# Seven products in place of eight in the first layer of five experts, with sums of w1 on GpSimd and running sums in PSUM

## The chip, the cores and the metric

The kernel runs on one core of a Trainium2 chip. The metric is the time of one execution in microseconds on the device, median of several runs; lower is better. Engines are called PE (TensorE, matmuls), ACT (ScalarE), DVE (VectorE), POOL (GpSimd) and SP (queue that issues most of the DMA).

## What is computed

An attention block with a decaying state (RWKV), whose result is regrouped into 3072 rows of 384, and then a mixture of eight experts in which every expert gets exactly 384 rows. Everything is float32.

```python
for t in range(S):                       # B=4, H=8, S=768, D=48
    cur = einsum('bhd,bhe->bhde', u * k[t], v[t])
    y[t] = einsum('bhd,bhde->bhe', r[t], state + cur)
    state = w * state + einsum('bhd,bhe->bhde', k[t], v[t])
x = y as (3072, 384)
logits = x @ w_gate                      # (3072, 8)
# all (row, expert) pairs from the largest logit down: the row goes to the expert
# if the row is free and the expert has fewer than 384 rows
for e in range(8):                       # w1 (8, 384, 1024), w2 (8, 1024, 384)
    h = maximum(x[mask_e] @ w1[e], 0)
    out[mask_e] = h @ w2[e]
```

## The kernel before

**Stages.** The first 125 us or so are attention (class `Mild`, an order written out by hand). The assignment of rows ("the walk", class `Assignment`) finds one expert's 384 rows after another: short steps on DVE with small matmuls on PE between them (tiles `counts`, `some_ps`, `list_ps`, `st_ps`; most of its DVE operations go through a helper at L930). The experts are computed in the order in which the walk finds them; n counts them in that order. Expert 0 is partly computed beside the end of attention (`early`), n = 1 to 7 by `Experts.run`, and at the end a piece of 128 rows that was put off (n = 8).

**One expert.** `fetch` gathers its 384 rows by three indirect DMAs of POOL (L1511) and loads w2 and w1 (1.5 MB each, L1504, in this order, on SP's queue). The buffers of weights and rows alternate between two pools, `turns[n % 2]`. `turn` transposes the rows to `xT`, three blocks of 128 inner indices by 384 rows (L1526), through PSUM and ACT (L1527). `hidden` computes the first layer transposed: for each of eight pieces of 128 hidden units three matmuls over the inner blocks (weights: a 128 x 128 block of w1; moving operand: 384 columns of xT) sum up in one bank of PSUM, and ACT takes the maximum with zero into `hid` (L1539, L1541).

**Second layer.** For n = 1 to 5, rows 0 to 255 go through `seven`: the product of a 2 x 2 division of the hidden rows and a 2 x 2 division of w2 by seven products of sums (Winograd's form of Strassen's method) in place of eight. The blocks are named h0 to h3 and w0 to w3; the sums are S1 to S4 (of hid) and T1 to T4 (of w2). Rows 256 to 383 go through `result` in the ordinary way. For n = 6 and 7 (`many`) all 384 rows go through `fifteen`: fifteen products in place of eighteen, with sums H and W. `sums_of` makes all these sums on DVE (L1591, 128 x 512, or 128 x 768 for T), `products` runs the matmuls into groups of one bank (`p_ps`, L1614), copies each group to `res` on ACT (L1618) and combines the products on DVE (L1623). Rows leave by indirect DMA of POOL (L1635).

**What sets the order.** Within the experts' part the Tile framework's planner puts every engine's instructions into a fixed order, by estimated readiness and with earlier code first; each engine then runs its own list in that order and waits by semaphores. `progress` says at which fraction of an expert's work (0 to 1 hidden layer, 1 to 2 second layer) a further step of the walk is put into the program (`due`); the list of steps is the generator `later`. The next expert's `fetch` is asked for at the head of the loop in `run`, its `turn` ahead of the last `result` (or, for `many`, when the list of `due` runs out).

**Banks of PSUM.** Three pools of two banks each: `ps_t` (transposes, `xT_ps`), `ps_h` (hidden layer, `h_ps`), `ps_o` (second layer, `p_ps` and `o_ps`, which share the tag `o_ps`).

## Time and profile before

| what | value |
|---|---|
| median of 3 runs | 398.21 us (397.88 to 398.33) |
| the profiled execution, its own time | 398.63 us |
| its span, first to last instruction | 396.9 us |
| granted clock of PE | 0.996 |
| PE busy | 381.1 us, 96% of the span |
| DVE, ACT, POOL busy | 267.4, 161.3, 137.9 us |
| first-layer passes of 384 columns (L1539) | 336, busy 114.9 us |
| second-layer passes of 192 columns (L1614) | 280 |
| second-layer passes of 128 columns (L1614) | 240 |

The page shows one execution. Busy times of different engines overlap; [...] the mean of one pass is longer than the distance from one pass to the next. A float32 matmul appears as two passes, each with its own load of weights (PEld).

### The profile page before, as it was taken

The page shows a single profiled execution, that of the slowest core. Times are in us where ns is not written, and L with a number is a line of the kernel's source. Part 1 is how long each engine was busy: PE and PEld are TensorE (multiplying, and loading weights), DVE is VectorE, ACT ScalarE, POOL GpSimd, SP SyncE. Part 2 cuts the span into 40 slices and gives each one's busy share as a digit, 9 for nine tenths or more (in the row PEclk, how much of TensorE's full clock was granted, in tenths as well). Part 3 has the DMA queues.
Part 4 walks back from the last instruction along what each step waited for, and adds up shares of the span by engine and source line. Part 5 has one row for each costly group of instructions (what it writes and reads, how often), then busy time and mean ns, then how long its engine had stood idle before and what let it go on. Part 6 is the DMA issues. An engine that isn't in the chain of part 4 may idle for free.

```text
span 396.9 us, 8692 instructions
## 1 busy us (share of the span) xinstructions
PE 381.1 (96%) x3243; PEld 289.4 (73%) x3243; DVE 267.4 (67%) x934; ACT 161.3 (41%) x429; POOL 137.9 (35%) x173
## 2 busy tenths in 40 slices
PE   7899999999999998999999999999999999999993
PEld 5678888888877764587578569558757857966981
DVE  6755777576885787967839819979578663952620
ACT  4997878888873311222222122221222222222220
POOL 7888877666732022031121120302303221040020
PEclk9999999999999999999999999999999999999998
DMA  9999999897692164641460650109209173370010
GB/s 121 158 184 205 197 201 171 151 177 153 125 327 81 42 247 169 215 164 40 152 246 12 220 208 2 60 0 334 84 21 359 57 281 120 99 300 2 2 61 26
DMA packets 95331, 57.29 MB, mean 144 GB/s; under 512 B 77232, under 2 KB 89520, under 8 KB 95280
## 3 DMA queue, kind: packets, MB, share of 16 engines
q1 hardware_dynamic: 91936, 47.21, 47.4%
q0 software_dynamic: 3104, 9.44, 6.7%
q8 instruction: 27, 0.44, 0.5%
q14 instruction: 24, 0.20, 0.2%
q10 hardware_dynamic: 240, 0.00, 0.0%
HBM read 47.20 MB, written 9.44 MB: 143 GB/s over the span
## 4 chain that ended last, share of the span: by engine, by line
PE 73%; DVE 10%; issue 4%; ACT 3%; POOL 3%; DMA 3%; SPq 1%; POOLq 0%; another core or an unknown queue 0%; DVEq 0%; ACTq 0%
PE h_ps L1539 26%; PE p_ps L1614 14%; PE o_ps L1641 7%; PE y_ps L542 6%; PE g_ps L504 4%; PE e_h_ps L1709 3%; PE kv_ps L521 2%; DMA krs<-in_k_dram 2%; PE kT_ps L458 2%; ACT AT L495 2%; PE x_ps L591 2%; PE lg_ps L571 2%; PE xT_ps L1526 2%; DVE W L1591 2%; PE rT_ps L458 1%
## 5 line engine op out<-in xcount | busy, mean ns | idle before, releaser
L1539 PE MATMUL h_ps<-xT,w 128*128 128x384 f32 (+1 forms) x384 | 120.8, 467 | 0.6 <-ACT e_o_sb L1721 0.6
L1539 PEld LDWEIGHTS h_ps<-xT,w 128*128 128x128 f32 x384 | 66.7, 190 | 39.1 <-issue 2.2
L1541 ACT ACTIVATE hid<-h_ps 128x384 f32<-128x384 f32 (+1 forms) x64 | 29.7, 464 | 91.3 <-PE h_ps L1539 79.9
L495 ACT ACTIVATE AT<-ident,dd 128x128 f32<-128x128 f32 x192 | 59.1, 391 | 2.0 <-DVE dd L448 1.8
L1511 POOL DMA_INDIRECT xg<-x_rows,tok x22 | 21.9, 997 | 88.0 <-issue 36.0
L1635 POOL DMA_INDIRECT out_dram<-o_all,to x16 | 17.6, 1103 | 99.2 <-DVE o_all L1623 66.8
L508 DVE COPY_PREDICATED AT<-mask,g_ps 128x512 f32<-128x512 uint8 x48 | 32.6, 732 | 12.1 <-PE g_ps L504 10.7
L1618 ACT COPY res<-p_ps 128x384 f32<-128x384 f32 (+2 forms) x28 | 13.2, 473 | 60.5 <-PE p_ps L1614 58.4
L1641 PE MATMUL o_ps<-w,hid 128*128 128x384 f32 x96 | 33.1, 488 | 0.0
L504 PE MATMUL g_ps<-rT,kT 48*128 48x128 f32 x384 | 27.9, 284 | 0.7 <-DVE AT L508 0.6
L436 POOL TENSOR_TENSOR kss<-krs,wk 128x384 f32<-128x384 f32 x24 | 24.3, 1017 | 8.0 <-DVE krs L340 5.5
L504 PEld LDWEIGHTS g_ps<-rT,kT 48*128 48x128 f32 x384 | 23.4, 187 | 4.0 <-PE unread_ps L418 0.5
L542 PE MATMUL y_ps<-AT,vts 128*64 128x128 f32 x384 | 25.7, 276 | 0.0
L443 POOL TENSOR_TENSOR rk<-rk,u_bc 128x384 f32<-128x384 f32 x24 | 24.2, 1007 | 1.9
L442 POOL TENSOR_TENSOR rk<-krs 128x384 f32<-128x384 f32 x24 | 24.6, 1024 | 0.2 <-DMA krs<-in_r_dram 0.2
L1641 PEld LDWEIGHTS o_ps<-w,hid 128*128 128x128 f32 x96 | 17.2, 190 | 9.5 <-issue 0.2
L542 PEld LDWEIGHTS y_ps<-AT,vts 128*64 128x64 f32 x384 | 20.6, 137 | 1.2 <-issue 0.7
L1614 PE MATMUL p_ps<-T,S 128*128 128x192 f32 x120 | 20.9, 328 | 0.0
L1591 DVE TENSOR_TENSOR H<-hid 128x512 f32<-128x512 f32 x12 | 7.9, 687 | 19.1 <-ACT hid L1541 19.1
L560 ACT COPY x<-y_ps 128x512 f32<-128x512 f32 x24 | 14.0, 585 | 14.6 <-PE y_ps L542 14.6
L1614 PEld LDWEIGHTS p_ps<-T,S 128*128 128x128 f32 x120 | 19.6, 190 | 0.1
L1614 PE MATMUL p_ps<-w,hid 128*128 128x192 f32 (+1 forms) x112 | 19.0, 316 | 0.0
(303 smaller groups left out, 684.9 us busy)
## 6 DMA issues: line engine op xcount, KB each, us to landing
w<-in_moe_w_dram SPq DMA_DIRECT2D x18, 1536.0 KB, 6.8
krs<-in_k_dram SPq DMA_DIRECT2D x24, 192.0 KB, 4.4
krs<-in_r_dram SPq DMA_DIRECT2D x24, 192.0 KB, 4.9
vts<-in_v_dram SPq DMA_DIRECT2D x24, 192.0 KB
x_rows<-xr SPq DMA_DIRECT2D x24, 192.0 KB, 3.0
xg<-x_rows,tok POOLq DMA_INDIRECT x22, 4.2
out_dram<-o_all,to POOLq DMA_INDIRECT x16, 2.7
out_dram<-o_sb,to POOLq DMA_INDIRECT x5
```

The costliest lines, as they stand in the source:

```text
L436: self.nc.gpsimd.tensor_mul(self.kss[:, n % self.NS].rearrange("p (g h) d -> p g h d", g=2)[:, :, :, 0:D], src, self.wk.rearrange("p (g h) ...
L442: nc.gpsimd.tensor_mul(rk, self.krs[:, n % self.NK, 1, 0:H, 0:D], self.krs[:, n % self.NK, 0, 0:H, 0:D])
L443: nc.gpsimd.tensor_mul(rk, rk, self.u_bc)
L495: nc.scalar.mul(AT[:, z, a, :], self.ident, dd[:, h:h + 1])
L504: nc.tensor.matmul(g_ps[:, z, a, :], kT[rows, a, :], rT[rows, a, :], start=True, stop=True)
L508: nc.vector.copy_predicated(out=AT[:, z], mask=self.mask.unsqueeze(1).to_broadcast([128, HP, T]), data=g_ps[:, z])
L542: nc.tensor.matmul(yv[q * PD:(q + 1) * PD, o // 2, o % 2, :], lhsT, rhs, start=(o // 2, q) not in seen, stop=stop, skip_group_check=True)
L1511: nc.gpsimd.indirect_dma_start(out=xg[:, c, :], out_offset=None, in_=x_dram[0:within, :], in_offset=bass.IndirectOffsetOnAxis(ap=tok[:, c: ...
L1539: nc.tensor.matmul(h_ps[:, 0:m], w1[:, f, ts(j, 128)], xT[:, f, 0:m], start=(f == 0), stop=(f == KD - 1))
L1541: nc.scalar.activation(hid[:, j, 0:m], h_ps[:, 0:m], AF.Relu)
L1614: nc.tensor.matmul(ps[:, q, :], left[a][:, j, :], right[b][:, j, :], start=(j == 0), stop=(j == KF // 2 - 1))
L1641: nc.tensor.matmul(o_ps, hid[:, j, ts(c, 128)], w2[:, j, :], start=(j == 0), stop=(j == KF - 1))
```

## The change

Five experts (`FIRST_BY_SEVEN`: n = 2, 3, 5, 6, 7) compute the first layer by `hidden_by_seven`. Inner blocks 0 and 1 of xT and of w1, halves of the rows (192 each, a0 to a3) and halves of the hidden units (512 each, b0 to b3) make a 2 x 2 by 2 x 2 product that is done by seven products; the third inner block (d0, d1 by c0, c1) is multiplied in the ordinary way, in the same accumulations. The hidden units are done in two passes p, each with half of them. One bank (A) takes P1, P6, P7 and P4 one after another as a running sum that is copied out by ACT between them; bank B takes P5 and P3, bank C takes P2. DVE adds what was kept to what stands in the bank for three of the four blocks.

The sums of w1 (T1 to T4, 128 x 512) are made on POOL during the second layer of the expert ahead, those of xT (S1 to S5, 128 x 192) on DVE after its `turn`.

The second layer's `seven` is rewritten with running sums in the same manner: P1, P6, P7 and P4 in one bank, P5 and P3 in another, P2 in a bank of `ps_t`; `turn` is now called ahead of P4. Four copies of ACT, one copy of the last block and three additions of DVE take the place of four copies and seven additions. T4 changes its sign.

For `fifteen` the products, the sums H and the combinations are the same in another order, and the two sums that were made after half of the hidden layer are made after all of it.

```diff
--- before.py
+++ after.py
...
+            self.first = pool("f_first", 1, **how)
...
+        def weight_sums(self, w1):
+            H = F // 2
+            at = {f"b{2 * k + f}": w1[:, k, ts(f, H)] for k in range(2) for f in range(2)}
+            at.update({f"c{f}": w1[:, 2, ts(f, H)] for f in range(2)})
+            for name, a, op, b in (("T1", "b1", SUB, "b0"), ("T2", "b3", SUB, "T1"), ("T3", "b3", SUB, "b1"),
+                                   ("T4", "b2", SUB, "T2")):
+                t = self.first.tile([128, H], F32, name=f"first_{name}")
+                nc.gpsimd.tensor_tensor(out=t, in0=at[a], in1=at[b], op=op)
+                at[name] = t
+            return at
+
+        def row_sums(self, xT):
+            H = CAP // 2
+            at = {f"a{2 * i + k}": xT[:, k, ts(i, H)] for i in range(2) for k in range(2)}
+            at.update({f"d{i}": xT[:, 2, ts(i, H)] for i in range(2)})
+            for name, a, op, b in (("S1", "a2", ADD, "a3"), ("S2", "S1", SUB, "a0"), ("S4", "a1", SUB, "S2"),
+                                   ("S5", "d0", SUB, "d1"), ("S3", "a0", SUB, "a2")):
+                t = self.first.tile([128, H], F32, name=f"first_{name}")
+                nc.vector.tensor_tensor(out=t, in0=at[a], in1=at[b], op=op)
+                at[name] = t
+            return at
+
+        FIRST = {"P1": (("a0", "b0"),), "P2": (("a1", "b2"), ("d0", "c0")), "P5": (("d1", "c1"), ("S1", "T1")),
+                 "P6": (("S2", "T2"),), "P7": (("S3", "T3"),), "P3": (("S5", "c1"), ("S4", "b3")),
+                 "P4": (("d1", "c0"), ("a3", "T4"))}
+        FIRST_ORDER = ("P1", 0), ("P2", 0), ("P5", 0), ("P6", 0), ("P1", 1), ("P7", 0), ("P3", 0), ("P4", 0), \
+            ("P5", 1), ("P6", 1), ("P2", 1), ("P7", 1), ("P3", 1), ("P4", 1)
+
+        def hidden_by_seven(self, x, w, progress):
+            hid = self.h.tile([128, KF, CAP], F32, name="hid")
+            Q, H = KF // 4, CAP // 2
+            banks, kept = {}, {}
+
+            def bank(p, which):
+                if (p, which) not in banks:
+                    pool, name, tag = {"A": (self.ps_h, "h_ps", None), "B": (self.ps_o, "hb_ps", "o_ps"),
+                                       "C": (self.ps_t, "hc_ps", "xT_ps")}[which]
+                    banks[p, which] = pool.tile([128, Q, H], F32, name=name, tag=tag or name), True
+                ps, fresh = banks[p, which]
+                banks[p, which] = ps, False
+                return ps, fresh
+
+            def keep(p, name, ps):
+                t = self.sums.tile([128, Q, H], F32, name=f"kept_{name}", tag=f"sum_False_{5 + 3 * p + len(kept) % 3}")
+                nc.scalar.copy(t, ps)
+                kept[name, p] = t
+
+            def block(p, i, f, src):
+                nc.scalar.activation(hid[:, ds(f * KF // 2 + p * Q, Q), ts(i, H)], src, AF.Relu)
+
+            def added(p, i, f, name, other):
+                t = kept[name, p]
+                nc.vector.tensor_tensor(out=t, in0=t, in1=other, op=ADD)
+                block(p, i, f, t)
+
+            for step, (name, p) in enumerate(self.FIRST_ORDER):
+                ps, fresh = bank(p, {"P2": "C", "P5": "B", "P3": "B"}.get(name, "A"))
+                pairs = self.FIRST[name]
+                for a, b in pairs:
+                    for q in range(Q):
+                        nc.tensor.matmul(ps[:, q, :], w[b][:, ts(p * Q + q, 128)], x[a], start=fresh,
+                                         stop=(a, b) == pairs[-1], skip_group_check=True)
+                        fresh = False
+                if name in ("P1", "P5", "P6"):
+                    keep(p, name, ps)
+                elif name == "P2":
+                    added(p, 0, 0, "P1", ps)
+                elif name == "P7":
+                    added(p, 1, 1, "P5", ps)
+                elif name == "P3":
+                    added(p, 0, 1, "P6", ps)
+                else:
+                    block(p, 1, 0, ps)
+                progress((step + 1) / len(self.FIRST_ORDER))
+            return hid
...
         SEVEN_EARLY = (("S3", "h0", SUB, "h2"),)
         SEVEN_LATE = (("S1", "h2", ADD, "h3"), ("S2", "S1", SUB, "h0"), ("S4", "h1", SUB, "S2"))
-        SEVEN = ((("p1", "h0", "w0"), ("p2", "h1", "w2")), (("p7", "S3", "T3"), ("p5", "S1", "T1")),
-                 (("p6", "S2", "T2"), ("p3", "S4", "w3")), (("p4", "h3", "T4"),))
-        SEVEN_OUT = ((("o0", "p1", ADD, "p2"),), (), (("u2", "p1", ADD, "p6"), ("u3", "u2", ADD, "p7"),
-                     ("u4", "u2", ADD, "p5"), ("o1", "u4", ADD, "p3"), ("o3", "u3", ADD, "p5")),
-                     (("o2", "u3", SUB, "p4"),))
-        EARLY_SUMS = (("H1", "h0", ADD, "h2"), ("H11", "h0", SUB, "h4"))
-        HID_SUMS = (("H8", "h1", ADD, "h3"), ("H7", "h1", SUB, "h0"), ("H9", "h1", SUB, "H11"),
-                    ("H3", "h5", SUB, "H9"), ("H0", "h1", ADD, "h2"), ("H6", "h3", ADD, "h5"),
+        SEVEN = (("P1", "h0", "w0"), ("P2", "h1", "w2"), ("P5", "S1", "T1"), ("P6", "S2", "T2"), ("P3", "S4", "w3"),
+                 ("P7", "S3", "T3"), ("P4", "h3", "T4"))
+        HID_SUMS = (("H7", "h1", SUB, "h0"), ("H8", "h1", ADD, "h3"), ("H6", "h3", ADD, "h5"), ("H1", "h0", ADD, "h2"),
+                    ("H11", "h0", SUB, "h4"), ("H9", "h1", SUB, "H11"), ("H3", "h5", SUB, "H9"), ("H0", "h1", ADD, "h2"),
                     ("H5", "H11", ADD, "H6"), ("H2", "h2", SUB, "H6"), ("H12", "H2", ADD, "h4"))
...
-        PRODUCTS = ((("p4", "h4", "w1"), ("p1", "H1", "w2"), ("p11", "H11", "W11"), ("p10", "h5", "w4")),
-                    (("p8", "H8", "w5"), ("p13", "h1", "W13"), ("p7", "H7", "W7"), ("p9", "H9", "W9")),
-                    (("p3", "H3", "w3"), ("p0", "H0", "W0"), ("p14", "h2", "W14"), ("p5", "H5", "W5")),
+        PRODUCTS = ((("p10", "h5", "w4"), ("p13", "h1", "W13"), ("p7", "H7", "W7"), ("p8", "H8", "w5")),
+                    (("p4", "h4", "w1"), ("p14", "h2", "W14"), ("p1", "H1", "w2"), ("p11", "H11", "W11")),
+                    (("p9", "H9", "W9"), ("p3", "H3", "w3"), ("p0", "H0", "W0"), ("p5", "H5", "W5")),
                     (("p12", "H12", "W12"), ("p6", "H6", "W6"), ("p2", "H2", "W2")))
...
-                              ("T4", "T2", SUB, "w2")), D)
+                              ("T4", "w2", SUB, "T2")), D)
...
-        def seven(self, left, right, tok, rows, at_product):
-            self.products(self.SEVEN, self.SEVEN_OUT, left, right, tok, rows, at_product, 2, 2)
+        def seven(self, left, right, tok, rows, at_product, between):
+            D = DX // 2
+            o_sb = self.o.tile([128, NC, DX], F32, name="o_all")
+            B = self.ps_o.tile([128, D], F32, name="pb_ps", tag="o_ps")
+            A = self.ps_o.tile([128, D], F32, name="pa_ps", tag="o_ps")
+            kept = {}
+
+            def added(i, k, name, ps):
+                nc.vector.tensor_tensor(out=o_sb[:, i, ts(k, D)], in0=kept[name], in1=ps, op=ADD)
+
+            for step, (name, a, b) in enumerate(self.SEVEN):
+                if name == "P2":
+                    ps = self.ps_t.tile([128, D], F32, name="pc_ps", tag="xT_ps")
+                else:
+                    ps = B if name in ("P5", "P3") else A
+                if name == "P4":
+                    between()
+                for j in range(KF // 2):
+                    nc.tensor.matmul(ps, left[a][:, j, :], right[b][:, j, :],
+                                     start=(j == 0 and name in ("P1", "P2", "P5")), stop=(j == KF // 2 - 1),
+                                     skip_group_check=True)
+                if name in ("P1", "P5", "P6", "P7"):
+                    kept[name] = self.sums.tile([128, D], F32, name=f"kept_{name}")
+                    nc.scalar.copy(kept[name], ps)
+                if name == "P2":
+                    added(0, 0, "P1", ps)
+                elif name == "P3":
+                    added(0, 1, "P6", ps)
+                elif name == "P7":
+                    added(1, 1, "P5", kept["P7"])
+                elif name == "P4":
+                    nc.scalar.copy(o_sb[:, 1, 0:D], ps)
+                at_product((step + 1) / len(self.SEVEN))
+            for c in range(2):
+                self.leave(o_sb[:, c, :], tok[:, c:c + 1], next(rows))
...
+        FIRST_BY_SEVEN = 2, 3, 5, 6, 7
...
+                after = ahead and ahead[0] in self.FIRST_BY_SEVEN and ahead[2].shape[1] == NC
...
+                def turn():
+                    nonlocal xT, row_sums
+                    if ahead:
+                        xT = self.turn(ahead)
+                        if after:
+                            row_sums = self.row_sums(xT)
+
                 def progress(t):
-                    nonlocal xT
+                    nonlocal weight_sums
+                    if after and t > 1.1 and not weight_sums:
+                        weight_sums = self.weight_sums(ahead[3])
                     while due and t > due[0]:
                         due.pop(0)
                         next(later, None)
-                        if many and not due and ahead:
-                            xT = self.turn(ahead)
+                        if many and not due:
+                            turn()
                 def at_product(part):
                     progress(1 + part)
-                hid = self.hidden(w1, xT, nb * 128, half if whole else lambda hid: None, progress)
+                if sums:
+                    hid = self.hidden_by_seven(sums, sums, progress)
+                    half(hid)
+                else:
+                    hid = self.hidden(w1, xT, nb * 128, half if whole else lambda hid: None, progress)
+                if many:
+                    self.sums_of(left, self.HID_SUMS)
+                    self.fifteen(left, right, tok, rows, at_product)
+                    continue
                 if whole:
-                    self.sums_of(left, self.HID_SUMS if many else self.SEVEN_LATE)
-                    (self.fifteen if many else self.seven)(left, right, tok, rows, at_product)
-                    if many:
-                        continue
+                    self.sums_of(left, self.SEVEN_LATE)
+                    self.seven(left, right, tok, rows, at_product, turn)
                 for c in range(NC - 1 if whole else 0, nb):
-                    if c == nb - 1 and ahead:
-                        xT = self.turn(ahead)
+                    if c == nb - 1 and not whole:
+                        turn()
                     self.result(c, hid, w2, tok, next(rows))
```

More of the change, by code (lines that the diff above doesn't have):

```diff
@@ L1561, in rwkv5_eagle_then_base_layer_balanced @@
                    ("W6", "W5", "w5"), ("W2", "W6", "w4"))
-        PRODUCTS = ((("p4", "h4", "w1"), ("p1", "H1", "w2"), ("p11", "H11", "W11"), ("p10", "h5", "w4")),
[2 rows of a table removed]
+        PRODUCTS = ((("p10", "h5", "w4"), ("p13", "h1", "W13"), ("p7", "H7", "W7"), ("p8", "H8", "w5")),
[2 rows of a table added]
                     (("p12", "H12", "W12"), ("p6", "H6", "W6"), ("p2", "H2", "W2")))
         OUT_SUMS = ((),
-                    (("x", "p9", SUB, "p4"), ("u", "x", SUB, "p7"), ("o0", "u", ADD, "p11"), ("t", "p13", SUB, "p11"),
-                     ("o1", "t", SUB, "x"), ("o7", "p10", ADD, "p4")),
-                    (("o6", "u", ADD, "p3"), ("y", "p13", ADD, "p14"), ("z", "y", SUB, "p0"), ("o2", "p1", SUB, "z"),
+                    (("t", "p13", SUB, "p11"), ("o7", "p10", ADD, "p4"), ("y", "p13", ADD, "p14")),
+                    (("x", "p9", SUB, "p4"), ("u", "x", SUB, "p7"), ("o0", "u", ADD, "p11"), ("o1", "t", SUB, "x"),
+                     ("o6", "u", ADD, "p3"), ("z", "y", SUB, "p0"), ("o2", "p1", SUB, "z"),
                      ("o5", "z", ADD, "p8"), ("d", "p11", SUB, "p5"), ("v", "p1", ADD, "d")),
@@ L1648, in result @@
             self.scatter(o_sb, tok[:, c:c + 1], to)
+        FIRST_BY_SEVEN = 2, 3, 5, 6, 7
         def run(self, ahead, later, rows, pulls={}, xT=None):
             xT, lead = xT or self.turn(ahead), True
+            row_sums = weight_sums = None
             while ahead:
@@ L1656, in run @@
                 many = whole and n in (E - 2, E - 1)
+                sums = dict(row_sums or {}, **weight_sums) if weight_sums else None
+                row_sums = weight_sums = None
                 ahead = next((a for a in later if a), None)
+                after = ahead and ahead[0] in self.FIRST_BY_SEVEN and ahead[2].shape[1] == NC
                 late, lead = lead and not many, False
@@ L1667, in half @@
                         left[name] = hid[:, ts(j, KF // 2), ts(i, 128)]
-                    last = self.sums_of(left, self.EARLY_SUMS if many else self.SEVEN_EARLY)
+                    if many:
+                        return
+                    last = self.sums_of(left, self.SEVEN_EARLY)
                     if late:
@@ L1677, in progress @@
                         next(later, None)
-                        if many and not due and ahead:
-                            xT = self.turn(ahead)
+                        if many and not due:
+                            turn()
                 def at_product(part):
                     progress(1 + part)
-                hid = self.hidden(w1, xT, nb * 128, half if whole else lambda hid: None, progress)
+                if sums:
[3 more added lines that the diff above has]
+                    hid = self.hidden(w1, xT, nb * 128, half if whole else lambda hid: None, progress)
+                if many:
+                    self.sums_of(left, self.HID_SUMS)
+                    self.fifteen(left, right, tok, rows, at_product)
+                    continue
                 if whole:
-                    self.sums_of(left, self.HID_SUMS if many else self.SEVEN_LATE)
-                    (self.fifteen if many else self.seven)(left, right, tok, rows, at_product)
-                    if many:
-                        continue
+                    self.sums_of(left, self.SEVEN_LATE)
+                    self.seven(left, right, tok, rows, at_product, turn)
                 for c in range(NC - 1 if whole else 0, nb):
-                    if c == nb - 1 and ahead:
-                        xT = self.turn(ahead)
+                    if c == nb - 1 and not whole:
+                        turn()
                     self.result(c, hid, w2, tok, next(rows))
```

## The prediction

> **What bounds the kernel now.** I read the page's busy shares first, then its slices, then the chain of waits in order of time, and last a table of stretches that I cut at the seams between experts.
>
> ```profile
> PE 381.1 (96%) x3243; PEld 289.4 (73%) x3243; DVE 267.4 (67%) x934; ACT 161.3 (41%) x429; POOL 137.9 (35%) x173
> ...
> PE   7899999999999998999999999999999999999993
> ...
> DVE  6755777576885787967839819979578663952620
> ```
>
> PE is busy in all slices from about 156 us (the experts) to 390 us. "Busy" could still hide gaps, so I take the spacing of matmuls from the chain (columns: start us, length us, what, how many). One fp32 matmul appears as two passes.
>
> ```profile
> 303.41 9.10 PE p_ps L1614 x56
> ...
> 352.36 13.01 PE h_ps L1539 x40
> ...
> 365.37 10.73 PE p_ps L1614 x96
> ```
>
> A pass over 384 columns takes 13.01/40 = 0.325 us, over 192 columns 9.10/56 = 0.1625, over 128 columns 10.73/96 = 0.112. A 192-column pass costs half of a 384-column one, although each carries its own weight load; halving the width costs nothing. Expert n's hidden layer (n=1 starts at 156.1, n=7 at 352.3) takes 48 x 0.325 = 15.6 us, which is what the stretches show: they have no room beyond a few walk matmuls. So the experts' stage is bound by PE from end to end.
>
> ```profile
> 173.00:188.90 15.90, 15.90 (x94) 13.23 (x92) 11.72 (x34) 3.58 (x8) 1.98 (x2) 1.00 0.12 42
> ...
> 205.30:221.40 16.10, 16.10 (x96) 13.32 (x93) 15.15 (x59) 3.59 (x8) 1.98 (x2) 1.00 0.07 26
> ...
> 303.40:318.70 15.30, 15.30 (x85) 13.02 (x84) 10.35 (x20) 3.58 (x9) 4.85 (x5) 1.00 0.39 149
> ...
> 335.20:352.30 17.10, 16.98 (x141) 15.41 (x139) 16.32 (x41) 3.98 (x9) 2.12 (x2) 1.00 0.50 175
> ```
>
> Columns after the length: PE, PEld, DVE, ACT and POOL busy us, clock, DMA share, GB/s. These are second layers of n=1, 2, 5 and 6. DVE is nearly full in n=2's (15.15 of 16.10, most of it the walk) and n=6's (16.32 of 17.10). In n=6's, though, some 6 us are n=7's w2 sums, done far ahead of need. POOL is almost idle.
>
> [...] The trace doesn't settle it: while POOL multiplies in attention, DVE's large operations read one operand from PSUM (L477, L508). The nearest sign is L340's copy, 0.20 us at the median and 0.57 at the most.
>
> [...]
>
> ```profile
> L442 POOL TENSOR_TENSOR rk<-krs 128x384 f32<-128x384 f32 x24 | 24.6, 1024 | 0.2 <-DMA krs<-in_r_dram 0.2
> ...
> L527 POOL TENSOR_TENSOR states<-states,chunk 128x192 f32<-128x192 f32 x16 | 8.2, 511 | 14.7 <-DVE states L526 10.6 <-DMA krs<-in_k_dram 2.8 <-DVE steps L882 1.4
> ```
>
> The mean column grows by 513 ns for 192 elements, so 512 elements take 1.37 us.
>
> [...]
>
> **The change, part by part.**
>
> *PE work of the first layer.* Before: 24 matmuls, 48 passes of 0.325 us = 15.6. After: the seven products hold 11 pairs; each runs over four 128-column pieces of w1, so 44 matmuls, 88 passes of 192 columns at 0.1625 = 14.3. That is 1.3 us less for each of experts 2, 3, 5, 6, 7: **-6.5 us**, all of it on the path. The second layer keeps its passes (56 or 120) in another order.
>
> *Running sums in the first layer.* Bank A takes P1, P6, P7, P4 in turn and must be read between. P6(0) is followed by only P1(1), 4 x 0.1625 = 0.65 us, before P7(0) writes A again. The copy needs the pass to end (0.33 from its start, L1614's mean, 0.16 after the next could issue), then 0.48 (L1618's 384-element copy): 0.65 us and the handovers. I take 0.08 us per expert, **+0.4** in all; the bounds are 0 (other matmuls fill it) and 1.0. P4(0) waits for DVE's addition after P7(0); it costs an interpolated 0.55 us (L526's 192 elements from PSUM 0.34, L477's 512 0.68) and P3 covers it with 1.3 us. If DVE is just in a 0.96 us T sum, P4 and everything behind it on PE waits up to 0.4.
>
> *DVE and ACT.* Per such expert, DVE gains six additions (6 x 0.55 = 3.3 us) in the hidden layer, and five row sums of 192 elements (0.35 each, 1.7) in the second layer of the expert before. Each seven second layer loses four of its seven output sums (4 x 0.35 = 1.4). DVE was busy 9.7, 6.2, 12.9, 7.3 and 2.3 us in the five hidden layers, of some 16, so it fits; but walk steps queue behind the additions, and PE holds their count matmuls in a fixed order. I take **+0.3** (0 to 3). For n=6 and 7 two H sums (1.4 us) move behind the hidden layer; the new order starts with h5 and h1, which need no sum and not the last block, and 11 sums at 0.6 spacing stay ahead of 15 products at 0.9: 0. ACT gains six copies of 0.48 us with four idle fifths: 0, unless its FIFO is late for P7.
>
> *Sums of w1 on POOL.* Four per expert, 4 x 1.37 = 5.5 us, 27 us over five. w1 lands at about 172, 204, 279, 308 and 330 us (end of each burst of DMA), before or early in the second layer of the expert ahead, so they are in time even for n=5, where 279 + 5.5 = 284.5 precedes 286.7. Behind them on POOL wait scatters of finished rows (needed by nobody until the end) and later gathers; the next gather is a full hidden layer off: 0. The cost is the lock. By w1's landing the sums fall on: n=1's second layer (DVE 11.72 of 15.9, some slack), n=2's (15.15 of 16.1, none), the ends of n=4's and n=5's (DVE light), and n=6's hidden layer (light). Unseen, so bounded: 0 if the lock isn't real; at most 5.5 each for n=1 and n=2, and 2.6 for the rest, 13.6, if DVE stands still and PE waits for all of it. [...] output sums saved are about paid back by row sums. I take 1.3 for n=2, 0.5 for n=1, 0.2 for the rest: **+2.0**.
>
> *The turn moved before P4.* The transposes of the next rows stand one product (1.3 us) earlier, ahead of 9 transposes that cover P7's copy. In n=4 the rows were barely there before: gathers issue at 274.6, 276.0 and 277.3, and land 4.2 us later (median), 278.8 to 281.5; PE transposes from 280.35. In n=5 PE also arrives 1.3 us sooner while the walk that finds the tokens keeps its pace. Late rows stop PE by up to 1.3 there and 2 us in n=5; nothing, if P4 and the third block's 5.2 us of matmuls are put ahead. I take **+0.3** (0 to 3.3).
>
> Sum: -6.5 + 0.4 + 0.3 + 2.0 + 0.3 = **-3.5 us**. The profiled execution took 398.63 us (span 396.9 and 1.7 around it), which would become 395.1; the median of the runs is 0.4 lower, 398.21, and gives **394.7**.
>
> **The rivals.**
>
> *Full gain.* The lock doesn't show or falls on DVE's slack, and the planner fills the bank waits: -6.5 and 0.4 of bank waits, 392.1. For it: PE has stood ready at nearly every seam so far, and DVE has slack in three of five places. Against it: n=2's 15.15 of 16.1.
>
> *Slower: [...]* 27 us of POOL sums block DVE's two-input sums, DVE comes late to the walk, and PE stands at the count matmuls, which it can't pass. It turns the sign once PE waits for over a quarter of POOL's time (6.5 of 27). At half, 13.5 - 6.5 = +7, 405; just past the point, 399 to 400. [...] Against it: w1 mostly lands where DVE is light.
>
> *It doesn't happen.* If an expert isn't full, the old path runs and nothing changes, 398.2. Against: L1614's 280 passes of 192 columns are 5 x 56, so experts 1 to 5 are full, and its 240 of 128 are 2 x 120, so are 6 and 7.
>
> **How the numbers follow.** About 0.2% (0.8 us) is what a measurement of this kernel can tell from no change. Forecast 0.55, full gain 0.24, POOL slower 0.16, nothing happens 0.05. The forecast's lower edge and the mildest form of the slower case put about 0.07 within 0.8 us of no change; that leaves 0.79 faster and 0.14 slower. The range takes in the full gain (391.8 is all of the 6.5) and the forecast with most of the lock's upper bounds, to 398.2.
>
> **What would show it.** Right: a new group of 192-column h_ps passes, 88 x 5 = 440, at 0.1625 us spacing; hidden layers of about 14.4 us for n=2, 3, 5, 6, 7; POOL sums of some 1.4 us each, 20 of them. The lock shows as DVE two-input sums longer than 0.69 (or 0.96) beside POOL sums, and as PE waiting for L930 in n=2's second layer. A late turn shows as PE idle before xT_ps. Wrong: PE idle that grows everywhere in the new hidden layers (the banks), or passes spaced wider than 0.17 us.

## Result and profile after

The changed kernel takes **407.41 us** (median of four executions, 406.14 to 407.96) against 398.23 us (397.88 to 398.33) for the kernel before: a ratio of 1.0226, 95% interval 1.0214 to 1.0238. It is 9.2 us slower. The profiled execution took 406.91 us, its span is 405.2 us and the granted clock 0.986 (before: 398.63, 396.9 and 0.996).

The page of the kernel after, first the busy shares, then the slices:

```profile
PE 381.7 (94%) x3443; PEld 320.2 (79%) x3443; DVE 299.1 (74%) x969; ACT 175.5 (43%) x464; POOL 170.0 (42%) x193
...
PE   8898999999999998979997999999999999979993
...
DVE  6854777576885788977978959978889995983630
...
PEclk9999999999999999999998999999999999989997
```

PE's line of nines now has three sevens, in the slices (10 us each) that begin at 172, 213 and 355 us, and in the second and third of these the clock has an 8. PE is no longer busy from end to end in the experts' part.

The stretches of the kernel after, cut from the first matmul of a layer to the first of the next (columns as before: length, PE, PEld, DVE, ACT, POOL, clock, DMA share, GB/s):

```profile
173.68:192.41 18.73, 16.21 (x93) 13.29 (x92) 15.02 (x35) 3.43 (x9) 8.27 (x7) 1.00 0.11 38
207.89:228.65 20.76, 18.33 (x97) 14.94 (x95) 18.40 (x53) 3.42 (x10) 7.99 (x6) 0.92 0.08 28
355.26:373.92 18.66, 16.36 (x96) 16.02 (x92) 10.20 (x36) 6.87 (x14) 7.71 (x4) 0.91 0.36 136
```

These are the second layers of n=1 and n=2, and the hidden layer of n=7. The second layers were shown before with 15.90 and 16.10 us of PE without a hole. POOL's share in them has gone from 2 to 8 us, DVE's from 11.72 and 15.15 to 15.02 and 18.40, and PE now stands idle 2.5 and 2.4 us. The table below has the same cut for all layers, in us, and for four experiments that are told further on:

| layer | before | after | e2: no sums of w1 | e1: sums on DVE | e3: sums alone | e6: second layer alone |
|---|---|---|---|---|---|---|
| second, n=1 | 15.94 | **18.73** | 16.13 | 16.76 | **18.44** | 16.12 |
| hidden, n=2 | 16.38 | 15.47 | 15.43 | 15.43 | 16.38 | 16.38 |
| second, n=2 | 16.14 | **20.76** | 16.73 | 16.38 | **19.62** | 16.36 |
| hidden, n=3 | 16.01 | 15.04 | 15.04 | 15.45 | 16.01 | 16.47 |
| second, n=3 | 16.56 | 16.50 | 16.50 | 16.50 | 16.56 | 16.52 |
| hidden, n=4 | 16.60 | 16.97 | 16.97 | 16.97 | 16.59 | 16.96 |
| second, n=4 | 16.04 | 16.48 | 16.30 | 16.54 | 16.22 | 16.15 |
| both, n=5 | 32.00 | 31.53 | 31.52 | 31.53 | 32.02 | 32.14 |
| hidden, n=6 | 15.97 | 15.39 | 14.88 | 15.43 | 15.96 | 15.97 |
| second, n=6 | 14.71 | 14.71 | 14.71 | 14.71 | 14.71 | 14.89 |
| hidden, n=7 | 15.97 | **18.66** | 15.10 | 15.42 | 16.03 | 16.29 |

Three layers lose 2.8, 4.6 and 2.7 us. All else together gains 1.8 (the other rows gain 2.2, the matmuls of the put-off piece 0.4, and the experts begin 0.8 later); that makes the 8.3 us between the two spans.

**The largest hole, n=2's second layer.** First PE's timeline of the kernel after (columns: start us, length us, what, how many, and in brackets the idle time before it and what ended it):

```profile
211.98 1.14 PE L1689 MATMUL pa_ps<-T,S 128*128 128x192 f32 x6
215.55 0.26 PE L942 MATMUL counts<-prop,ind 128*128 128x64 bf16 x3 [2.43 <-DVE ind L930]
```

PE stops in the middle of a product, because its fixed order has a walk matmul (`counts`) there and DVE has not made `ind`. The bracket counts from the modelled end of the last pass before the hole. The next pass could have followed 0.163 us after the start of that one, which is 0.16 us earlier; idle times of PE that the text names without a line count from there (this one is 2.59 us). Then DVE's timeline for the same time:

```profile
211.62 0.98 DVE L1043 TENSOR_SCALAR full<-most 128x16 f32<-128x16 f32 x1
212.63 0.17 DVE L1045 TENSOR_REDUCE dg<-full 128x1 f32<-128x16 f32 x1
212.84 0.98 DVE L1047 SCALAR_TENSOR_TENSOR cand<-cell,dg,base 128x16 f32<-128x16 f32 x1
213.75 1.28 DVE L1050 SCALAR_TENSOR_TENSOR low<-cell,dg,low 128x1 f32<-128x1 f32 x1
214.95 0.54 DVE L930 TENSOR_TENSOR ind<-m,cand 128x384 bf16<-128x384 f32 x1
215.42 1.23 DVE L1039 TENSOR_SCALAR base<-cells,low 128x16 f32<-128x16 f32 x1
```

and POOL's:

```profile
210.72 3.07 POOL L1542 TENSOR_TENSOR first_T<-w 128x512 f32<-128x512 f32 x2 [4.47 <-PE counts L953]
213.75 2.87 POOL L1542 TENSOR_TENSOR first_T<-w,first_T 128x512 f32<-128x512 f32 x2
```

The same steps of the kernel before, in the same layer:

```profile
208.06 0.17 DVE L1043 TENSOR_SCALAR full<-most 128x16 f32<-128x16 f32 x1
...
208.47 0.23 DVE L1047 SCALAR_TENSOR_TENSOR cand<-cell,dg,base 128x16 f32<-128x16 f32 x1
208.62 0.22 DVE L1050 SCALAR_TENSOR_TENSOR low<-cell,dg,low 128x1 f32<-128x1 f32 x1
...
209.49 0.23 DVE L1039 TENSOR_SCALAR base<-cells,low 128x16 f32<-128x16 f32 x1
```

So L1043, L1047, L1050 and L1039 took 0.17, 0.23, 0.22 and 0.23 us before; here they take 0.98, 0.98, 1.28 and 1.23. L1043 and L1039 read one tensor; L1047 and L1050 (`scalar_tensor_tensor`) read two, both in SBUF. Taken one by one, POOL's sums start at 210.72, 212.53, 213.75 and 215.09 and last 1.85, 1.26, 1.26 and 1.53 us, so they end at 212.57, 213.79, 215.01 and 216.62. The four DVE operations end at 212.60, 213.82, 215.03 and 216.65. Each of these tiny steps has waited for the end of one POOL sum: it ends 0.02 or 0.03 us after it. The reduction between them (0.17) and `ind` (0.54; 0.56 before) did not wait. Three of the four stand ahead of `ind` and add 2.62 us; PE's wait is 2.43 us by the line (2.59 by the other count).

**After the hole PE runs at half its clock.** Stretches of the kernel after, columns as above:

```profile
213.10:215.50 2.40, 0.02 (x1) 0.00 (x0) 2.40 (x4) 0.00 (x0) 2.32 (x3) 1.00 0.00 0
215.50:216.70 1.20, 1.15 (x9) 1.15 (x10) 1.20 (x2) 0.32 (x1) 1.12 (x1) 0.99 0.05 14
216.70:220.00 3.30, 3.30 (x13) 3.13 (x12) 2.56 (x6) 0.00 (x0) 0.34 (x1) 0.50 0.01 2
...
357.20:359.70 2.50, 0.26 (x2) 0.00 (x0) 2.50 (x13) 0.00 (x0) 2.50 (x1) 1.00 0.93 369
...
360.20:363.00 2.80, 2.80 (x11) 2.80 (x10) 2.49 (x11) 0.42 (x2) 2.22 (x2) 0.50 0.39 142
```

From 216.7 to 220.1 us the clock is 0.50; the 16 passes from 215.65 to 220.02 take 4.37 us where 16 x 0.163 = 2.6 would do, so this costs another 1.8 us. The same happens once more, from 360.0 to 363.4, after the hole at n=7: 12 passes take 3.71 us in place of 2.0, 1.7 us more. That is what the two clock digits of the page show. Busy PE at half clock looks the same in the busy slices.

**n=1 and n=7.** At n=1 the hole is 2.68 us before `counts`, with DVE's sums of hid at 1.64 and 1.62 us beside POOL's sums (0.69 in the kernel before). At n=7 the delay began 19 us earlier, at the start of n=6's second layer: four POOL sums run from 338.08 to 344.09, and DVE's first six sums H come late.

```profile
340.60 5.84 DVE L1664 TENSOR_TENSOR H<-hid 128x512 f32<-128x512 f32 x6 [0.59 <-ACT hid L1583]
...
359.21 0.17 DVE L930 TENSOR_TENSOR some<-some_ps,quarter 128x16 f32<-128x16 f32 x1
...
359.54 0.17 DVE L1415 TENSOR_REDUCE part<-some 128x4 f16<-128x16 f32 x1
```

Six sums at 0.6 us spacing would be 3.7; the second and third took 1.75 us each beside POOL's, of 1.75 and 1.71. In e2 (below), where POOL has no sums, DVE runs the same list in the same order. Counted from the start of n=6's second layer, DVE comes to the fourth sum at 1.86 us there and at 4.00 here, 2.14 later, and to the walk step `some` at 16.72 there and 18.65 here, still 1.93 later: DVE has too few pauses on the way to catch up. The matmul for `some` had ended at 355.4; PE's list matmul, which needs `part`, starts at 359.76 after a hole of 2.46 us.

**What went as planned.** Lines by shape of the kernel after (busy us, mean ns), and one product of the new hidden layer:

```profile
L1542 POOL TENSOR_TENSOR first_T<-w 128x512 f32<-128x512 f32 x10 | 14.9, 1507 | 8.1 <-PE counts L953 4.5 <-DMA w<-in_moe_w_dram 3.6
L1542 POOL TENSOR_TENSOR first_T<-w,first_T 128x512 f32<-128x512 f32 x10 | 14.3, 1425 | 0.3
```

```profile
198.35 1.46 PE L1595 MATMUL hb_ps<-first_S,w 128*128 128x192 f32 x8
199.65 0.49 PE L1595 MATMUL hb_ps<-xT,w 128*128 128x192 f32 x2
```

POOL's 20 sums are there at 1.47 us on the mean (1.26 at the least). ACT's 30 copies from banks in the middle of a running sum (L1579) take 0.48 us at the median, as taken; that a bank can be read there was an assumption of the author that no trace of the kernel before shows. Eight passes from 198.35 to 199.65 are 0.163 us each: the narrow passes are as cheap as assumed, and where nothing stops PE the hidden layers are 15.0 to 15.5 us in place of 16.0 to 16.4.

### The profile page after: what moved, and what is told of

It reads as the page before. It is cut to its first block, busy times and chain, and to the rows that moved or that the text cites. A ratio compares the mean times of both kernels' runs of the same rounds, so it can differ in the third digit from the quotient of the medians.

```text
span 405.2 us, 9267 instructions
## 1 busy us (share of the span) xinstructions
PE 381.7 (94%) x3443; PEld 320.2 (79%) x3443; DVE 299.1 (74%) x969; ACT 175.5 (43%) x464; POOL 170.0 (42%) x193
## 5 line engine op out<-in xcount | busy, mean ns | idle before, releaser
L1741 POOL DMA_INDIRECT out_dram<-o_all,to x16 | 20.7, 1296 | 65.6 <-DVE o_all L1729 35.8
L1616 PE MATMUL h_ps<-xT,w 128*128 128x384 f32 (+1 forms) x144 | 39.0, 423 | 0.6 <-ACT e_o_sb L1850 0.6
L1616 PEld LDWEIGHTS h_ps<-xT,w 128*128 128x128 f32 x144 | 22.6, 191 | 11.3 <-ACT e_o_sb L1850 1.2
L1583 ACT ACTIVATE hid<-kept_P 128x384 f32<-128x384 f32 x30 | 15.7, 523 | 24.7 <-DVE kept_P L1587 24.1
L1618 ACT ACTIVATE hid<-h_ps 128x384 f32<-128x384 f32 (+1 forms) x24 | 10.1, 420 | 29.0 <-PE h_ps L1616 24.7
L477 DVE TENSOR_TENSOR rT<-rT_ps,WR 112x512 f32<-112x512 f32 x23 | 15.7, 685 | 4.6 <-PE rT_ps L458 4.6
L1542 POOL TENSOR_TENSOR first_T<-w 128x512 f32<-128x512 f32 x10 | 14.9, 1507 | 8.1 <-PE counts L953 4.5
L448 DVE TENSOR_REDUCE dd<-rk 128x8 f32<-128x384 f32 x24 | 13.1, 546 | 6.9 <-POOL rk L443 6.9
L1595 PE MATMUL h_ps<-first_S,first_T 128*128 128x192 f32 x80 | 17.5, 342 | 0.0
```

Of the source, the lines that this page charges most:

```text
L1595: nc.tensor.matmul(ps[:, q, :], w[b][:, ts(p * Q + q, 128)], x[a], start=fresh, stop=(a, b) == pairs[-1], skip_group_check=True)
L1616: nc.tensor.matmul(h_ps[:, 0:m], w1[:, f, ts(j, 128)], xT[:, f, 0:m], start=(f == 0), stop=(f == KD - 1))
L1741: nc.gpsimd.indirect_dma_start(out=to, out_offset=bass.IndirectOffsetOnAxis(ap=tok, axis=0), in_=o_sb, in_offset=None)
```

## Experiments

The theory after the result (A, the theory of the lock): POOL's sums hold back DVE, DVE is late for the walk, PE waits and then pays again at half clock (0.50 after the holes at n=2 and n=7). By the lock is meant that a DVE operation waits until a POOL sum beside it has ended, as the 0.98 us of L1043 in place of 0.17 show it; for the prediction it was an assumption of the author, which the kernel before doesn't show. The rival: the running sums in PSUM make PE wait, or the rewritten order of the second layer does. Times are medians; ratios are against runs of the kernel before on the same chip.

**e1: the same sums on DVE.**

```diff
-                nc.gpsimd.tensor_tensor(out=t, in0=at[a], in1=at[b], op=op)
+                nc.vector.tensor_tensor(out=t, in0=at[a], in1=at[b], op=op)
```

> The changed kernel with the 20 sums of w1 on DVE instead of POOL, at the same place in the program. Theory A ([...] DVE comes late to the walk, PE stands at the walk's matmuls [...]): the three gaps of 2.5 to 2.7 us go; DVE gets 4 x 0.6 = 2.4 us more per expert, which costs something where it is full (n=2, n=6): 394 to 400 us. Theory B (it is DVE's own added work and the waits for banks that cost the time): slower still than the changed kernel's 407.4, since DVE gets 12 us more: 410 to 416.

Measured: 398.28 us, ratio 1.0002 (0.9993 to 1.0010). The 20 sums take 0.68 us each on DVE, 13.7 us in all, half of what they take on POOL, and the three bad layers are back at 16.76, 16.38 and 15.42 us. Moving 29 us of work from an idle engine to the second busiest one saves 9.1 us.

**e2: no sums.** The products read plain blocks of w1.

```diff
-                t = self.first.tile([128, H], F32, name=f"first_{name}")
-                nc.gpsimd.tensor_tensor(out=t, in0=at[a], in1=at[b], op=op)
-                at[name] = t
+                at[name] = at[a]
```

> The changed kernel without the sums of w1: the products take blocks of w1 in place of T1 to T4 (that part of the computation is left out); all else stays. A: without POOL sums the five hidden layers keep their 0.9 to 1.0 us each: 393 to 395 us, no gap over 1 us on PE, clock 0.99 or more. B: still 402 us or more.

Measured: 395.43 us, ratio 0.9932 (0.9915 to 0.9948). So the sums on POOL cost 407.41 - 395.43 = 12.0 us; on DVE they cost 2.9. The time is 0.4 us over the expected range; the holes of over 1 us are gone, and the clock is 0.998, as expected. What is left of the change without any sums gains 2.9 us.

**e3: the sums alone.** The kernel before, with the 20 POOL sums and nothing that reads them.

```diff
+                t = self.first.tile([128, H], F32, name=f"first_{name}")
+                nc.gpsimd.tensor_tensor(out=t, in0=at[a], in1=at[b], op=op)
...
+                    if after and t > 1.1 and not weight_sums:
+                        weight_sums = self.weight_sums(ahead[3])
```

> The kernel before with only the 20 sums of w1 on POOL added, in the places where the change has them; nobody reads them. A: PE gaps behind the walk at n=1 and n=2, as in the changed kernel, and DVE's tail at n=6: 404 to 409 us. B: the sums lie on an idle engine and nobody waits: 398 to 399 us.

Measured: 405.64 us, ratio 1.0206 (1.0173 to 1.0239). Nothing waits for these sums, and they cost 7.3 us, in the second layers of n=1 and n=2 (18.44 and 19.62 us). (The profiled execution was the shortest of the four, 404.50 us, so its layers account for 5.9 of the 7.3.) DVE's timeline of this kernel in n=2's second layer:

```profile
208.44 1.15 DVE L1604 TENSOR_TENSOR S<-hid 128x512 f32<-128x512 f32 x1
209.52 1.34 DVE L930 TENSOR_TENSOR wide<-digit_of,cnt 128x128 f16<-128x128 f32 x1
210.78 1.75 DVE L1604 TENSOR_TENSOR S<-S,hid 128x512 f32<-128x512 f32 x1
```

POOL's four sums run from 207.78 to 213.67. Here they met the operations with two inputs (0.69 becomes 1.15 to 1.75, `wide` 0.29 becomes 1.34), and L1043, which comes after them, is at 0.16 again. PE has holes of 1.42 and 2.07 us before the two `counts`, and 2.57 us before n=1's. All of them end on DVE's `wide` or `ind`, none on a gather of POOL, so it isn't POOL's being late with its own work that PE waits for. The theory of the lock stands without any part of the running sums. The third loss, at n=7, was expected here too and is not there (16.03 us).

**e4: only two experts,** those whose sums fall on a lightly loaded DVE.

```diff
-        FIRST_BY_SEVEN = 2, 3, 5, 6, 7
+        FIRST_BY_SEVEN = 5, 6
```

> The changed kernel with FIRST_BY_SEVEN = 5, 6: POOL's sums only in the second layers of n=4 and n=5, where DVE has little to do. A: two savings of 0.5 to 0.9 us, no large gap: 396.5 to 398. B: two fifths of the 9.2 us lost: 401 to 403.

Measured: 399.35 us, ratio 1.0028 (1.0017 to 1.0040). That missed. The sums did little harm here (n=4's second layer is 0.16 us longer than in e6), but the second layer is rewritten in this kernel too, and something in it costs more than the two experts gain. That led to e6.

**e5: POOL only writes.** Three clears of the same size in place of each sum in e3, so that POOL is as long busy (0.47 us a clear, 1.41 for three, where a sum of e3 takes 1.42 on the mean) but reads nothing from SBUF.

```diff
+                for _ in range(3):
+                    nc.gpsimd.memset(t, 0.0)
```

> The kernel before with POOL memsets (three of 512 elements for each of the 20 sums, about 1.5 us together) in the places where e3 has the sums; nobody reads them. If the cost of e3 comes from what POOL reads from SBUF [...], memsets cost next to nothing: 398 to 399.5 us and no gap over 1 us at the walk's matmuls. If it comes from POOL's being occupied (gathers and scatters late), they cost what the sums cost: 404 to 407.

Measured: 419.06 us, ratio 1.0523 (1.0491 to 1.0555): missed by both theories. The clears do not read w1, so they came early and in long rows (22, then 31, then 7), and as a like-for-like of time the experiment is lost. Its rows tell more than its time. First DVE in both long rows, then POOL in the second:

```profile
159.89 0.22 DVE L1064 SCALAR_TENSOR_TENSOR fills<-dge,dg,first_e 128x8 f32<-128x8 f32 x1
160.03 8.05 DVE L1067 TENSOR_SCALAR past<-m,value 128x24 f32<-128x24 f32 x1
...
187.01 0.96 DVE L1605 TENSOR_TENSOR T<-w 128x768 f32<-128x768 f32 x1 [0.39 <-PE p_ps L1628]
...
188.21 9.19 DVE L1043 TENSOR_SCALAR full<-most 128x16 f32<-128x16 f32 x1
```

```profile
182.83 14.53 POOL L1542 MEMSET first_T<- 128x512 f32 x31
```

The sum with two inputs beside the clears has its old 0.96 us, and the `scalar_tensor_tensor`, which reads two tensors of SBUF as well, its old 0.22. But two `tensor_scalar` operations on 16 and 24 elements take 9.19 and 8.05 us in place of 0.17 and 0.23; the first ends at 197.40, with the last clear of its row (197.36), the second at 168.08 (168.05). So two cases are to be told apart here: operations with two SBUF inputs waited beside POOL's sums, which read SBUF (0.98 and 1.28 us in place of 0.23 and 0.22 in the kernel after, 1.15 to 1.75 in place of 0.69 in e3), and not beside its clears, which only write (0.22 and 0.96); `tensor_scalar` from SBUF to SBUF waited beside both (0.98 in place of 0.17 beside a sum, 9.19 beside clears). And a wait lasted over many POOL instructions that follow each other: some 19 clears went by in the 9.19 us. It needn't: in n=2's second layer above, each of the four steps got in after one sum (0.98 to 1.28 us), with the next sum starting within 0.08 us. What decides this was not found.

**e6: the second layer alone.** No expert uses the new first layer.

```diff
-        FIRST_BY_SEVEN = 2, 3, 5, 6, 7
+        FIRST_BY_SEVEN = ()
```

> The changed kernel with FIRST_BY_SEVEN empty: all first layers as before, only the second layer rewritten (running sums, turn ahead of P4, the new order of the fifteen). If the rewritten second layer is neutral, as I had it: 398 to 398.6. If it costs what e2 and e4 leave open (the seams of n=2 to 4 were 0.2 to 0.6 us longer there): 399 to 400.

Measured: 400.31 us, ratio 1.0049 (1.0033 to 1.0066): the rewritten second layer costs 2.1 us, a little over the second expectation. By the table it is spread: 0.46 in n=3's hidden layer, 0.36 in n=4's, 0.32 in n=7's, and 0.1 to 0.2 in most second layers. In the three hidden layers PE waits before a walk matmul (`some_ps` for DVE's `vals`, 0.46 and 0.35; `list_ps` for `part`, 0.60): DVE's order has changed with the code's, and these walk steps come later than PE needs them. Which single move of it does this was not separated.

**e7: each sum on the engine that suits its place.** n=2, 3 and 7 on DVE, n=5 and 6 on POOL.

```diff
-                        weight_sums = self.weight_sums(ahead[3])
+                        weight_sums = self.weight_sums(ahead[3], nc.gpsimd if ahead[0] in (5, 6) else nc.vector)
```

> The changed kernel with the sums of w1 for n=2, 3 and 7 on DVE and those for n=5 and 6 on POOL, where DVE is light. Lock theory: the POOL sums cost little there, and DVE is spared 4.8 us: 397 to 398, a little under e1's 398.3. Rival: DVE is not what limits any more, same as e1: 398.3.

Measured: 397.79 us, ratio 0.9991 (0.9982 to 1.0000), the fastest version with all the sums, ahead of the kernel before by less than the 0.2% that counts as a difference here. PE waits 1.26 us before the transposes of n=5's rows, which have not landed.

**e8: e2 with the turn in its old place,** ahead of the last `result`.

```diff
-                    self.seven(left, right, tok, rows, at_product, turn)
+                    self.seven(left, right, tok, rows, at_product, lambda: None)
...
-                    if c == nb - 1 and not whole:
+                    if c == nb - 1:
```

> e2 (no sums of w1, blocks of w1 in their place) with the turn moved back behind the seven products, ahead of the last result, as in the kernel before. If the earlier turn meets rows that have not landed (e2 shows 0.64 us at n=4): 394.5 to 395. If P4 then waits bare for P7's copy, five times 0.4 us: 396 to 397.5.

Measured: 395.38 us, ratio 0.9926 (0.9910 to 0.9943), the same as e2 (395.43), and between the two expectations. The hole of 0.64 us at n=4's seam is gone, and as much has come up in small waits elsewhere.

**e9, e10, e11: the old seven products of the second layer under the new first layer** (`fifteen` keeps its new order), with the sums on DVE, mixed as in e7, or on POOL.

```diff
-        def seven(self, left, right, tok, rows, at_product, between):
...
+        def seven(self, left, right, tok, rows, at_product):
+            self.products(self.SEVEN, self.SEVEN_OUT, left, right, tok, rows, at_product, 2, 2)
...
-            res = self.sums.tile([128, count + own, D], F32, name=f"res{count}")
+            res = self.sums.tile([128, count + own, D], F32, name=f"res{count}", tag="res")
```

> The changed kernel with the second layer's seven products as before (products, old order, combinations on DVE, turn ahead of the last result; res of seven and of fifteen share one buffer to fit) and the sums of w1 on DVE. e6 says that the rewritten second layer costs 2.0 us. If that is the seven's rewriting: 2 us under e1's 398.3, so 396 to 397. If it is the new order of the fifteen: 398 to 398.5.

> The same with the sums for n=5 and 6 on POOL, those for n=2, 3 and 7 on DVE. If e7's gain of 0.5 us over e1 adds up: 395.5 to 396.5, which would beat the kernel before and the changed one. If the old turn and POOL's sums meet at n=4: as e9.

> The same with all sums on POOL: the change without its second-layer part. Lock theory: PE gaps of 2 us and more at n=1 and n=2 stay, 404 to 407. If the lock needs the rewritten second layer to bite: 398 or less.

Measured, beside 399.14 us for the kernel before on this chip: e9 398.94 us (ratio 1.0006, 0.9994 to 1.0017), e10 399.22 (1.0004, 0.9995 to 1.0013), e11 405.70 (1.0182, 1.0154 to 1.0210). e11 came out as the theory of the lock has it: n=1's and n=2's second layers are at 18.89 and 20.45 us, and the same kernel with the sums on DVE (e9) is 6.8 us faster. e9 missed, and e10 is where e9 is: the 2.1 us of e6 do not come back. In e9 n=4's layers are at 16.59 and 16.04 us again, as before, but n=6's hidden layer has grown to 16.91. PE's timeline of e9 there, and then DVE's:

```profile
333.41 0.92 PE L1595 MATMUL h_ps<-xT,w 128*128 128x192 f32 x4 [1.75 <-DVE kept_P L1587]
```

```profile
331.73 0.69 DVE L1542 TENSOR_TENSOR first_T<-w 128x512 f32<-128x512 f32 x1 [5.71 <-PE hb_ps L1595]
332.34 0.55 DVE L1587 TENSOR_TENSOR kept_P<-kept_P,hc_ps 128x384 f32<-128x384 f32 x1
332.81 0.55 DVE L1587 TENSOR_TENSOR kept_P<-kept_P,h_ps 128x384 f32<-128x384 f32 x1
```

DVE has been idle for 5.71 us. The first operation of its list is a sum of n=7's w1, whose transfer has only just ended (the DMA is 90% busy or more from 321 until about 331); two additions stand behind it that could have run, and PE waits for the second of them to hand back bank A. The trace names a PE instruction as what ended the wait. But the sum reads only w1, and the last product that read the buffer it writes had ended at 327.8; the last packet of w1 ended at 331.07. e1 has the same order with a hole of 0.45 us, and there the trace names the transfer of w. In e10's profiled execution the trouble comes from POOL again (it is the longest of 13, 400.65 us, so it shows more than the median does): its sums of n=6's w1 run from 310.07 to 316.11, three output sums take 4.11 us in place of about 0.9, and PE waits 1.97 us for `vals` at 324.58 and then runs at half clock (0.61 on the mean from 325.1 to 328.4, 0.84 from there to 331). So a gain of one part was lost at another seam: the costs of the parts do not add up. In both traces the loss goes through DVE's one list.

**e12: e7 with the turn in its old place,** the edits of e7 and e8 together.

> The changed kernel with two edits together: the sums of w1 on DVE for n = 2, 3 and 7 and on POOL for n = 5 and 6, and the turn back in its old place, ahead of the result of the last 128 rows. With the turn ahead of P4 and the same engines (e7) the time was 397.79 us, and PE stood 1.26 us at n=4 before the transposes of rows that had not landed. If that wait is a loss of its own, the old place takes it away: 396.6 to 397.4, faster than the kernel before by 0.2 to 0.4%. If the turn's place only moves waits about, as it did without any sums (e8: no net difference), 397.6 to 398.0 and the wait turns up elsewhere. If a seam's transposes now come too late for the next hidden layer: over 398.2.

Measured: 399.19 us, ratio 1.0022 (1.0011 to 1.0033), slower than e7 by 1.4. That is the time of the third expectation, but not its reason. The wait for the rows is gone, and others are there: 1.53 us before `counts` at 289.79 and 1.04 us before bank A at 334.29 (DVE again idle 4.84 us for n=7's w1). DVE's timeline of e12 shows what made the first:

```profile
278.85 5.07 DVE L1664 TENSOR_TENSOR T<-w 128x768 f32<-128x768 f32 x1 [0.88 <-PE pa_ps L1689]
```

One sum of w2 took 5.07 us in place of 0.96 beside POOL's sums of n=5's w1 (279.37 to 285.04). In e7 the same sum took 3.74 us, and PE was waiting for rows just then. The sums on POOL are not harmless at n=4 either; that PE's wait for the rows covered them in e7 fits the times, but was not tested. No kernel here with all the sums is clearly faster than the kernel before.

## Why the prediction was wrong

The forecast was -3.5 us and the result is +9.2. Of the rivals it was the slower one that came true, in what it said of DVE's sums (0.69 us became 1.64 at n=1) and in its place: PE at matmuls of the walk, which it can't pass (the count matmuls at n=1 and n=2, the list matmul at n=7). Its point, PE waiting for more than 6.5 of POOL's 27 us, was passed: the sums cost 12.0 of 29.2 us, 3.5 of them by the clock.

- **The lock, taken as 2.0 us (1.3 at n=2, 0.5 at n=1, 0.2 for the rest): the step that failed.** e3 shows 7.3 us with nothing else changed; in its profiled execution 3.5 at n=2, 2.5 at n=1, and under 0.3 at any other layer. In the change it is 12.0. Three things were wrong with the term. It priced DVE's large sums alone, but L1043 and L1039, `tensor_scalar` with one input, stopped for a POOL sum each (0.98 and 1.23 us in place of 0.17 and 0.23), as did the small L1047 and L1050 with two (0.98 and 1.28 in place of 0.23 and 0.22). It spread the delay over DVE's slack by busy time; n=1's layer had 4 us of slack and PE still lost 2.5, since the walk steps form one chain with PE (matmul, DVE steps, matmul), whose delay is not made up by slack at another time. And "the rest" included n=6's hidden layer as light, whereas the six H sums that follow it meet two POOL sums, and DVE's list carries the 2 us on until 359 us. (On how long one POOL sum takes, the term was near: taken as 1.37 us, it is 1.26 undisturbed and 1.47 on the mean.)
- **PE's clock, in no term.** About 1.8 us at n=2 and 1.7 at n=7, 3.5 of the 12.0. e3's profiled execution, whose clock stays at 1.00 through its holes, has none of it; its three other executions, with clocks of 0.987 to 0.991, took 1.0 to 3.6 us longer.
- **The second layer, taken as 0.** "The second layer keeps its passes in another order" is true of PE, and e6 is +2.1. The order of DVE's list, which moves with the code, was not costed.
- **PE's passes, taken as -6.5.** From the start of one pass to that of the next it is 0.3225 us for 384 columns and 0.1625 for 192, so 48 x 0.3225 - 88 x 0.1625 = 1.18 an expert, 5.9 in all. The 0.325 of the prediction, 13.01 us over 40 passes, counts the last pass to its end, which the profile puts 0.17 us after the start of the next one (one pass of 384 columns is 0.494 us long there on the mean); that made 0.6 us too much. Realised without the sums of w1 (hidden layers of n=2, 3, 6, 7 and all of n=5): 4.4 in e2 against the kernel before, 5.3 against e6, whose layers have longer waits for the walk. So bank waits, DVE's additions and walk waits together took 0.6 to 1.5, where the forecast had 0.4 + 0.3; they were not separated. DVE's additions were 0.55 us each, as interpolated.
- **The turn, +0.3.** Without sums its place makes no difference (e8 against e2, 0.05 us). What was named, rows that land late at n=4, is there: 0.64 us in e2, 0.83 in the kernel after, 1.26 in e7.

By parts, in medians: second layer +2.1 (e6), first layer without sums of w1 -4.9 (e2 less e6), sums on POOL +12.0 (the change less e2); together +9.2, as they must, since the three differences form one chain.

Of the signs that the prediction gave, "DVE two-input sums longer than 0.69 (or 0.96) beside POOL sums, and PE waiting for L930 in n=2's second layer" are both there. The waits view of the kernel after:

```profile
PE counts L942 <- DVE ind L930: 3.9, 4, 2.4
PE counts L953 <- DVE wide L930: 2.5, 1, 2.5
PE list_ps L1424 <- DVE part L1415: 2.3, 1, 2.3
```

These are us in total, times, and the longest; the kernel before had 1.7 us for the first, 0.7 at the longest, and the others are not in its list.

## What to carry to other kernels

POOL being idle does not make it free: an elementwise sum there took twice DVE's time (1.47 us, 0.68 in e1) and held up DVE's operations with two SBUF inputs (0.69 became up to 1.75 in e3) and its `tensor_scalar` steps (0.17 became 0.98), so ask first what short DVE steps run at that time and whether PE waits for them; on DVE itself the same sums cost a quarter (2.9 us in e1 against 12.0). A chain that goes to and fro between PE and DVE has to be costed by its own steps, not by DVE's busy share, and a hole on PE like those of 1.97 to 2.6 us here is to be priced with the half clock that may follow (another 1.7 to 1.8 us here). When code is moved, look also at what then stands first in an in-order list: a sum that waits for a transfer holds up everything behind it (e9).

## What was not expected of the hardware

**The half clock came in whole steps of 3.413 us.** In the record of the granted clock of all 14 traces every full-clock stretch lasts a whole number of steps of 3.413 us (114 in the kernel before; 61, 41 and 11 in the kernel after), and every half-clock stretch within the experts lasts one step, or two or three (e5: 6.83 and 10.24 us). The two of the kernel after run from 216.68 to 220.09 and from 360.04 to 363.45 us; their starts are 143.36 us apart, which is 42 x 3.413. With that grid laid over the holes, it fits which of them are punished: n=2's hole fills 0.67 of one step and n=7's 0.72, e11's at n=2 0.69, e10's at n=6 0.58, and the next step runs at half clock. n=1's hole in the kernel after is longer, 2.68 us, but falls on two steps (0.40 and 0.38), and the clock stays; e11's of 3.03 us splits into 0.36 and 0.53. The edge isn't sharp by this measure: the highest share without a penalty was 0.58 as well (e3; by the profile's own ends e10's is 0.53). Against the program's start the grid lies differently from trace to trace (a step begins 0.12 us after a whole number of steps in e3, 1.64 in the kernel after, 3.28 in e7). That executions of one kernel differ fits this: three of e9's 13, with a clock of 0.992, took 400.5 to 400.8 us, the others 398.4 to 399.5.

**A DVE operation was held off by a row of POOL instructions,** not by one alone: 9.19 us behind clears (e5), 3.75 us for a sum of 0.96 in the kernel after, 5.07 in e12. Small `tensor_scalar` steps, on 16 and 24 elements a row, were held even where POOL only writes (9.19 and 8.05 us in e5); `scalar_tensor_tensor`, down to one element a row, was held beside POOL's sums (1.28 us in place of 0.22) and not beside its clears (0.22).
